# Layer scale, x + gamma * y: HBM in two blocks of 64 rows, and y's first rows on two DMA rings

## The chip, the core and the metric

The kernel runs on one core of one Trainium2 chip. The metric is the device time of one execution in microseconds (us). Before the change the median of 3 runs is 119.68 us (119.56 to 119.86).

## The reference

```python
B, S, D = 1024, 16, 512          # bf16
def reference(x, y, gamma):      # x, y: (B, S, D), gamma: (D,)
    return x + gamma * y
```

x and y are read once and the result is written once: 16.8 MB each, 50.3 MB in all.

## The kernel before

The 16,384 rows of 512 elements (1 KB each) are seen as 128 rows on each of 128 partitions. "Row" below means one such row on every partition, 128 KB in all. The whole of y lies in SBUF (`y_sb`, 128 rows a partition), and the result is made in place there. x passes through a smaller buffer, `x_sb`, of 76 rows, so the later part of x overwrites rows that have been added already.

`BLOCKS` says how HBM is cut: in a block of n rows each partition's n rows lie next to each other, so a transfer of part of a block is one contiguous run for each partition (4 rows: 4,096 B; 64 rows: 65,536 B). `PIECES` says how the rows are cut for VectorE (DVE). There is no scheduler; the lists at the top are the order:

- `SP` is what SyncE issues on its DMA ring, in order: y's rows 0 to 4, y's rows 4 to 68, x's rows 4 to 68, y's rows 68 to 128, x's rows 68 to 120, x's rows 120 to 128. The fourth number of an x entry is the row of `x_sb` where it goes.
- `ACT` is what ScalarE issues on its ring: x's rows 0 to 4, gamma (1 KB), and the three stores. ScalarE computes nothing.
- `EARLY` takes the first two entries of SP and the first of ACT ahead of the program's opening barrier (the last lines of the kernel function move these instructions to the front of the main block).
- `HOLD` and `AHEAD`: all entries of a ring after its first (2, 1) wait until the transfer `HOLD`, y's rows 0 to 4, has landed. TensorE (PE) waits for that landing and passes it on to SP, ACT and DVE.
- An x entry that overwrites rows of `x_sb` waits for the adds that read them (`frees`). In before.py x's rows 68 to 120 wait for the first add, of 44 rows, and x's rows 120 to 128 wait for the later ones.
- `RELEASE`: the first store waits, besides for its adds, until x's rows 68 to 120 have landed (`s_go`), so that nearly all reads come before all writes.
- `DVE` is the order of the multiplies (m) and adds (a) by piece. A multiply waits for the y transfers that its piece touches, an add for its x transfers.

gamma is spread over the partitions by a matmul of PE with a row of ones (line 152), and DVE casts it to bf16 (line 154). PE takes the landing of `HOLD` first, then waits for gamma. The first multiply (line 180) can't start before the cast. The adds are line 189. The DMA instructions are issued in `ring`: gamma at line 129, x at 132, y at 135, the stores at 138. Each DMA is spread over 16 DMA engines, 8 partitions each, and its landing counts 16 completions.

Of the kernel before, what the change touches and what calls it, by code (L numbers as in the profile page):

```python
# [3 lines left out]

BLOCKS = [4, 64, 60]

PIECES = [8, 16, 44, 52, 8]


SP = [
    ('y', 0, 4),
    ('y', 4, 68),
    ('x', 4, 68, 4),
    ('y', 68, 128),
    ('x', 68, 120, 24),
    ('x', 120, 128, 0),
]
ACT = [('x', 0, 4, 0), ('g',), ('s', 4, 68), ('s', 0, 4), ('s', 68, 128)]  # L20

EARLY = (2, 1)

HOLD, AHEAD = ('y', 0, 4), (2, 1)

RELEASE = ('x', 68, 120, 24)

DVE = [('m', 0), ('m', 1), ('m', 2), ('a', 2), ('a', 0), ('a', 1), ('m', 3), ('m', 4), ('a', 3), ('a', 4)]
MULT, ADD = mybir.AluOpType.mult, mybir.AluOpType.add


def _take(sem, n, eng):


    return eng.wait_ge(sem, n).then_inc(sem, -n)  # L35


def kernel(
# [18 lines left out]
    rows = N // P  # L57
    n = len(PIECES)
    assert sum(PIECES) == rows
    starts = [sum(PIECES[:c]) for c in range(n + 1)]  # L60
    dt = xf.dtype
    edges = [sum(BLOCKS[:c]) for c in range(len(BLOCKS) + 1)]
    assert edges[-1] == rows

    def rows_of(t, a, b):

        c = max(c for c in range(len(BLOCKS)) if edges[c] <= a)
        assert b <= edges[c + 1]
# [6 lines left out]
    y_sb = nc.alloc_sbuf_tensor("y_sb", [P, rows, D], dt).ap()  # L75
    x_loads = [w for w in ACT + SP if w[0] == "x"]
    y_loads = [w for w in SP + ACT if w[0] == "y"]
    stores = [w for w in SP + ACT if w[0] == "s"]
    for loads in (x_loads, y_loads, stores):
# [9 lines left out]
    s_add, s_go, s_rel, s_end, s_out = sem("s_add"), sem("s_go"), sem("s_rel"), sem("s_end"), sem("s_out")  # L89
    added = [a for kind, *a in DVE if kind == "a"]  # L90
    order = {a[0]: k for k, a in enumerate(added)}

    def meets(a, b, c, d):
        return a < d and c < b
# [4 lines left out]
    def x_at(row):  # L99
        return next(w[3] + row - w[1] for w in x_loads if w[1] <= row < w[2])  # L100
# [12 lines left out]
    def ring(eng, what, n_early, n_ahead):  # L113

        known, went = 0, False
        for k, w in enumerate(what):
            kind = w[0]
            if k == n_ahead:
                _take(s_held[eng], 1, eng)
            need = frees(w) if kind == "x" else pieces_of(w[1], w[2]) + list(w[3:]) if kind == "s" else []  # L120
            need = max((order[c] + 1 for c in need), default=0)
            if kind == "s" and not went:
                _take(s_go, 1, eng)
                went = True
            if need > known:
                eng.wait_ge(s_add, need)
                known = need
            if kind == "g":
                i = eng.dma_start(out=gamma_row, in_=gamma.unsqueeze(0)).then_inc(s_gamma, 16)
            elif kind == "x":  # L130
                to = x_sb[:, w[3] : w[3] + w[2] - w[1], :]
                i = eng.dma_start(out=to, in_=rows_of(xf, w[1], w[2])).then_inc(s_load[w], 16)
            elif kind == "y":
                r = slice(w[1], w[2])
                i = eng.dma_start(out=y_sb[:, r, :], in_=rows_of(yf, w[1], w[2])).then_inc(s_load[w], 16)
            else:
                r = slice(w[1], w[2])
                i = eng.dma_start(out=rows_of(of, w[1], w[2]), in_=y_sb[:, r, :]).then_inc(s_out, 16)
            if k < n_early:
                early.append(i.ins)  # L140

    ring(nc.sync, SP, EARLY[0], AHEAD[0])
    ring(nc.scalar, ACT, EARLY[1], AHEAD[1])

# [11 lines left out]

    _take(s_load[RELEASE], 16, nc.tensor)
    nc.tensor.sem_inc(s_go, 1)
# [4 lines left out]
    def need(loads, c):  # L163
        for w in loads:
            if w not in landed and meets(starts[c], starts[c + 1], w[1], w[2]):
                if w == RELEASE:
                    _take(s_rel, 1, nc.vector)
                elif w == HOLD:
                    _take(s_held[nc.vector], 1, nc.vector)
                else:  # L170
                    _take(s_load[w], 16, nc.vector)
                landed.add(w)

    for kind, *args in DVE:
        c = args[0]
        yt = y_sb[:, starts[c] : starts[c + 1], :]
        if kind == "m":
            need(y_loads, c)
            g = gamma_sb[:, None, :].to_broadcast([P, PIECES[c], D])
            nc.vector.tensor_tensor(out=yt, in0=yt, in1=g, op=MULT).then_inc(s_dve, 1)  # L180
            open_mults += 1
        else:
# [4 lines left out]
            at = x_at(starts[c])  # L187
            xt = x_sb[:, at : at + PIECES[c], :]
            nc.vector.tensor_tensor(out=yt, in0=xt, in1=yt, op=ADD).then_inc(s_add, 1)  # L189
# [44 lines left out]
```

## Time and profile before

| | |
|---|---|
| median of 3 runs | 119.68 us |
| span of the profiled execution (first to last instruction) | 118.2 us |
| around the span, median less span | 1.5 us |
| bytes read, written | 33.56 MB, 16.78 MB; 426 GB/s over the span |
| DMA packets | 1442 (161 of them under 512 B: mostly completions) |
| VectorE busy | 70.1 us, 59% of the span, 12 instructions |
| TensorE busy | 0.6 us, one matmul |
| granted clock | 1.000 |

The span is the one that the profile was taken from; its device time is not listed beside it, so the difference between the median of the runs and the span stands for what lies around the span.

How to read it: DMA-issuing instructions are not counted as busy time of an engine; the work of the DMA engines is seen in the line of 40 slices (busy tenths of 16 engines) and in the table of queues (packets, MB, share of 16 engines' time). A packet is counted where it starts, with all of its bytes: the slices of a stretch with 64 KB packets therefore jump up and down, though the engines work evenly. In a list of instructions SPq and ACTq are the queues that issue DMAs, and the bracket at the end of a line tells how long the engine stood idle before it and what ended that.

| transfer | ring | issued at us | us to landing |
|---|---|---|---|
| y 0 to 4 | SP | 0.0 | 3.4 |
| y 4 to 68 | SP | 0.4 | 23.4 |
| x 0 to 4 | ACT | 0.1 | 4.2 |
| x 4 to 68 | SP | 3.7 | 39.5 |
| gamma | ACT | 3.9 | |
| y 68 to 128 | SP | 4.1 | 57.3 |
| x 68 to 120 | SP | 55.4 | 21.7 |
| x 120 to 128 | SP | 57.6 | 22.0 |
| store 4 to 68 | ACT | 77.4 | 23.8 |
| store 0 to 4 | ACT | 77.8 | 22.3 |
| store 68 to 128 | ACT | 94.4 | 21.5 |

### The profile page before, as it was taken

Reading aid. Unit: us, or ns where it says so; the run is one execution under the profiler, and the core shown is the slowest. Engines: PE = TensorE matmul, PEld = TensorE weight load, DVE = VectorE, ACT = ScalarE, POOL = GpSimd, SP = SyncE. Lnnn points to the kernel's source line nnn. Section 1 sums busy time; section 2 is a strip of 40 time slices with the busy share of each in tenths; the row PEclk is TensorE's granted clock in tenths of the full one; section 3 lists DMA queues with packets and bytes.
Section 4 is the critical chain, followed back from the end, with each engine's and each line's share of the span. In section 5 each row is a group of like instructions: output and inputs, shape, how many; then the busy total and the mean of one; then the engine's idle time right before and its main releaser. Section 6 shows DMA issues by size and latency. Waiting matters only on the chain. (4 is left out here: it accounts for less than half of the span.)

```text
span 118.2 us, 91 instructions
## 1 busy us (share of the span) xinstructions
PE 0.6 (0%) x1; PEld 0.1 (0%) x1; DVE 70.1 (59%) x12; POOL 0.2 (0%) x4
## 2 busy tenths in 40 slices
PE   0000100000000000000000000000000000000000
PEld 0000000000000000000000000000000000000000
DVE  0000200089999969999999999999999900000000
POOL 0000000000000000000000000000000000000000
DMA  6999889988899879879969696898899889799793
GB/s 248 461 666 399 355 355 399 665 355 355 355 599 466 355 333 624 374 333 499 499 288 576 288 576 288 360 637 355 355 576 488 355 355 510 333 582 416 333 499 166
DMA packets 1442, 50.33 MB, mean 426 GB/s; under 512 B 161, under 2 KB 162, under 8 KB 546
## 3 DMA queue, kind: packets, MB, share of 16 engines
q1 hardware_dynamic: 864, 33.03, 64.8%
q10 hardware_dynamic: 578, 17.30, 33.9%
HBM read 33.56 MB, written 16.78 MB: 426 GB/s over the span
## 5 line engine op out<-in xcount | busy, mean ns | idle before, releaser
L180 DVE TENSOR_TENSOR y_sb<-y_sb,gamma_sb 128x4096 bf16<-128x4096 bf16 (+3 forms) x5 | 34.7, 6981 | 10.9 <-DVEq L35 10.9
L189 DVE TENSOR_TENSOR y_sb<-x_sb,y_sb 128x4096 bf16<-128x4096 bf16 (+3 forms) x5 | 34.7, 6981 | 1.2 <-DVEq L35 1.1
L154 DVE CAST gamma_sb<-gamma_ps 128x512 bf16<-128x512 f32 x1 | 0.7, 692 | 10.2 <-DVEq L35 10.2
L146 DVE MEMSET ones_row<- 1x128 bf16 x1 | 0.2, 165 | 2.0 <-PEq L51 2.0
L152 PE MATMUL gamma_ps<-gamma_row,ones_row 1*128 1x512 bf16 x1 | 0.6, 581 | 11.6 <-PEq L35 11.6
L152 PEld LDWEIGHTS gamma_ps<-gamma_row,ones_row 1*128 1x128 bf16 x1 | 0.1, 101 | 11.6 <-issue 11.6
L218 POOL MEMSET const-bfloat16-1.0<- 128x1 bf16 x1 | 0.1, 101 | 0.0
L218 POOL MEMSET const-uint8-127<- 128x1 uint8 x1 | 0.1, 101 | 0.0
L218 POOL MEMSET const-float32-0.0<- 128x1 f32 x1 | 0.1, 98 | 0.2 <-issue 0.2
L218 POOL MEMSET const-float32-1.0<- 128x1 f32 x1 | 0.1, 98 | 0.0
## 6 DMA issues: line engine op xcount, KB each, us to landing
y_sb<-in_y_dram SPq DMA_DIRECT2D x1, 7680.0 KB, 57.3
out_dram<-y_sb ACTq DMA_DIRECT2D x1, 7680.0 KB, 23.8
x_sb<-in_x_dram SPq DMA_DIRECT2D x1, 6656.0 KB, 21.7
x_sb<-in_x_dram SPq DMA_DIRECT2D x1, 1024.0 KB, 22.0
y_sb<-in_y_dram SPq DMA_DIRECT2D x1, 512.0 KB, 3.4
x_sb<-in_x_dram ACTq DMA_DIRECT2D x1, 512.0 KB, 4.2
out_dram<-y_sb ACTq DMA_DIRECT2D x1, 512.0 KB, 22.3
y_sb<-in_y_dram SPq DMA_DIRECT2D x1, 23.4
```

Source lines behind the costliest of these rows:

```text
L146: nc.vector.memset(ones_row, 1.0).then_inc(s_ones, 1)
L152: nc.tensor.matmul(gamma_ps, ones_row, gamma_row, start=True, stop=True).then_inc(s_ps, 1)
L154: nc.vector.tensor_copy(out=gamma_sb, in_=gamma_ps).then_inc(s_dve, 1)
L180: nc.vector.tensor_tensor(out=yt, in0=yt, in1=g, op=MULT).then_inc(s_dve, 1)
L189: nc.vector.tensor_tensor(out=yt, in0=xt, in1=yt, op=ADD).then_inc(s_add, 1)
L218: nc = _bacc.Bacc("TRN2", target_bir_lowering=False, num_devices=1)
```

## The change

HBM is cut in two blocks of 64 rows. y's first block comes in two transfers: its first 8 rows as the only early entry on SP's ring, its next 56 rows as the first instruction on ACT's ring, ahead of gamma. `HOLD` is y's first 8 rows. x comes in 64, 56 and 8 rows, all on SP; there are two stores of 64 rows instead of three. DVE has four pieces, 20, 44, 56 and 8 rows, instead of five. Nothing below the lists is changed; line numbers fall by one.

```diff
-BLOCKS = [4, 64, 60]
-
-PIECES = [8, 16, 44, 52, 8]
+BLOCKS = [64, 64]
+
+PIECES = [20, 44, 56, 8]
 SP = [
-    ('y', 0, 4),
-    ('y', 4, 68),
-    ('x', 4, 68, 4),
-    ('y', 68, 128),
-    ('x', 68, 120, 24),
+    ('y', 0, 8),
+    ('x', 0, 64, 0),
+    ('y', 64, 128),
+    ('x', 64, 120, 20),
     ('x', 120, 128, 0),
 ]
-ACT = [('x', 0, 4, 0), ('g',), ('s', 4, 68), ('s', 0, 4), ('s', 68, 128)]
-
-EARLY = (2, 1)
-
-HOLD, AHEAD = ('y', 0, 4), (2, 1)
-
-RELEASE = ('x', 68, 120, 24)
-
-DVE = [('m', 0), ('m', 1), ('m', 2), ('a', 2), ('a', 0), ('a', 1), ('m', 3), ('m', 4), ('a', 3), ('a', 4)]
+ACT = [('y', 8, 64), ('g',), ('s', 0, 64), ('s', 64, 128)]
+
+EARLY = (1, 1)
+
+HOLD, AHEAD = ('y', 0, 8), (1, 1)
+
+RELEASE = ('x', 64, 120, 20)
+
+DVE = [('m', 0), ('m', 1), ('a', 1), ('a', 0), ('m', 2), ('m', 3), ('a', 2), ('a', 3)]
```

What each engine waits for after the change follows from the same rules: SP's x 0 to 64 waits for the landing of y 0 to 8, with y 64 to 128 behind it; x 64 to 120 goes to rows 20 to 76 of `x_sb` and waits for the first add (piece 1, rows 20 to 64); x 120 to 128 goes to rows 0 to 8 and waits for the second add (piece 0). The first multiply needs both early y transfers and gamma.

## The prediction

> **What bounds the kernel now.** I read the page's table of queues first, then the 40 slices, then the timeline, then the packet counts of short windows.
>
> ```profile
> DMA  6999889988899879879969696898899889799793
> ...
> q1 hardware_dynamic: 864, 33.03, 64.8%
> q10 hardware_dynamic: 578, 17.30, 33.9%
> ```
>
> The columns of the two queue lines are packets, MB and share of 16 engines' span; q1 is SP's ring and q10 ACT's. Together the packets fill 98.7% of the span, so the DMA engines bound the kernel, and nothing can be gained but the 1.0 us before the first packet and some tenths of packet overhead. Much can be lost: any stretch in which both rings are empty is added to the end. So the question is whether the change opens such stretches. The packet records give the prices: a run of 4,096 B takes an engine 0.159 us, 8,192 B 0.309, 53,248 B 1.966, 61,440 B 2.267 and 65,536 B 2.418 (57,344 B, which before.py lacks, falls at 2.117 between its neighbours).
>
> Next, who else is close. The timeline:
>
> ```profile
> 3.71 0.33 SPq L132 DMA_DIRECT2D x_sb<-in_x_dram  x1
> 3.90 0.50 ACTq L129 DMA_DIRECT2D gamma_row<-in_gamma_dram  x1
> ...
> 12.32 0.69 DVE L154 CAST gamma_sb<-gamma_ps 128x512 bf16<-128x512 f32 x1 [10.16 <-DVEq L35]
> 23.95 18.43 DVE L180 TENSOR_TENSOR y_sb<-y_sb,gamma_sb 128x4096 bf16<-128x4096 bf16 x3 [10.94 <-DVEq L35]
> 43.45 18.43 DVE L189 TENSOR_TENSOR y_sb<-x_sb,y_sb 128x22528 bf16<-128x22528 bf16 x3 [1.08 <-DVEq L35]
> ```
>
> Columns: start, length, engine, line. DVE starts at 23.95, when y's first 64-row transfer lands; gamma was ready at 13.01. From there DVE stands still for only 1.08 us (x's 64 rows) and ends its last add at 94.39; the last store is issued at 94.43. The transfer ahead of that store ends near 99.6 on the engines, and a store needs 1.32 us from issue to first packet (77.41 to 78.73), so **DVE has about 3.8 us to spare**: its start may slip from 23.95 to about 27.8 before the last store is late.
>
> **How two rings share an engine.** The change puts two long transfers on two rings at the start, so I need the sharing rule. Packet counts of three windows, 1.0 to 2.2, 2.2 to 3.05 and 3.05 to 3.65 us:
>
> ```profile
> q1 hardware_dynamic: 102, 0.42, 91.9%
> ```
> ```profile
> q10 hardware_dynamic: 60, 0.25, 72.8%
> q1 hardware_dynamic: 42, 0.11, 31.4%
> ```
> ```profile
> q10 hardware_dynamic: 62, 0.25, 101.4%
> ```
>
> In the first only y's rows 0 to 4 run (102 of 128 rows). ACT's x rows, issued at 0.13, come in at 2.2. In the second, chained end to end on one engine, the records read x, y, x, completion, x: one for one. On nearly every engine seven y rows (28 KB) were through before the first x row. y's 64 rows, third in the order of issue, start only after the last x row, at 3.65.
>
> Gamma shows the same with big packets. The windows 6.0 to 8.6, 8.6 to 8.65 and 11.1 to 11.15 us:
>
> ```profile
> q1 hardware_dynamic: 19, 1.25, 111.0%
> ```
> ```profile
> q10 hardware_dynamic: 1, 0.00, 5.8%
> ```
> ```profile
> q10 hardware_dynamic: 1, 0.00, 1.1%
> ```
>
> Gamma, issued at 3.90, waits behind the 64 KB packet that began at 6.1 (taken up ahead of it), goes at 8.62, and its completion, a packet of its own, waits for one more 64 KB packet until 11.12. So engines **alternate packet by packet whatever the size**, with one packet taken up ahead.
>
> [...]
>
> **The change, part by part.** "y8" is y 0:8 on SP, "y56" is y 8:64 on ACT; x64, y64, x56, x8 follow on SP.
>
> 1. Start. y8 stands where y's 4 rows stood, so it starts at 1.0 to 1.25; y56 stands where x's 4 rows stood, so it comes in after 28 KB of y8, which is 3.5 packets of 8 KB: four packets go first, four remain. From about 2.6 on the slowest engine the order is y56, y8, y56, y8, ... : the completion of y8 comes after five 56 KB packets and four of 8 KB, 5 x 2.117 + 4 x 0.309 = 11.8 us, at 14.4. (From above: eight packets first, 4.0 us. From below: two first, 19.)
>
> 2. The hold. PE passes y8's landing on; SP's x64 waits for it, with y64 queued behind, and ACT's gamma, with the stores behind. From last completion to x64's issue it took 0.66 us (3.05 to 3.71), so x64 is issued at 15.1, gamma at 15.3 (at 3.71 and 3.90 before, where y's 64 rows stood ahead of the hold and kept SP's ring full); x64's first packet is ready 1.0 (as y's first) to 1.3 us (as the store) later, 16.1 to 16.4.
>
> 3. Gamma. It is now **behind y56 in the same ring**. At 14.4 two or three packets of y56 remain: the sixth to 16.5, the seventh (taken up ahead) to 18.6, then turns: x64 to 21.0, y56's eighth to 23.2, x64 to 25.6, y56's completion, x64 to 28.0, gamma, x64 to 30.4, gamma's completion. An engine that began earlier is 0.3 ahead: 30.3. In before.py it was 1.9 us from there to the end of the cast (11.12 to 13.01), so DVE starts at 32.2. This is the step with most in it: if y56's completion goes together with its last packet, one turn of 2.4 us less; if x64 comes in before the seventh packet, 2.4 more.
>
> 4. DVE. A row costs 0.267 us and an operation 0.143 besides ((14.021 - 11.886)/8; 11.886 - 44 x 0.267). Pieces 20, 44, 56, 8: 5.48, 11.89, 15.09, 2.29, twice, 69.5; ten operations now sum to 69.8 and take 69.3 end to end, 0.05 less each; so 69.1. Two operations fewer save 0.2. Nothing lies idle in it: x64 lands at 40.5, before 49.5 when its add can begin; y64 lands at 59.8, wanted at 67.
>
> 5. x56. It overwrites x rows 20 to 64, so it waits for the add of 44 rows: issue at 32.2 + 29.1 = 61.3, first packet 62.4. y64's last packet ends at 59.4: **the rings are empty for 3.0 us**. Before, x's 52 rows were issued at 55.37, with 5 us of y still to come: that was the cover.
>
> 6. Stores. x56 lands at 79.8, x8's packets end at 81.9, and the first 64-row store follows to 101.3. The last add ends at 32.2 + 69.1 = 101.3; the second store is issued 0.04 later and its first packet goes at 102.6: another 1.3 us empty.
>
> 7. Packets. y's 4, x's 4 and the store of 4 rows go: 24 packets of 4 KB an engine, each 0.008 us longer than its bytes cost in a 64 KB packet, 0.2 us saved; one issue fewer on SP and one on ACT lie under transfers. Blocks of 64 rows leave each partition one run of up to 64 KB, a size that before.py's x, y and store already have at 2.418 us: nothing. It costs nothing also that x_sb shrinks to the same 76 rows.
>
> Sum, along DVE: 32.2 + 69.1 + 0.04 + 1.32 + 8 x 2.418 + 0.44 (spread of the engines) + 0.38 (last completion 117.84 to the end, 118.2) = 122.8, against the profiled 118.2: 4.6 more, which the two empty stretches (4.3) and the spread explain. The median of the runs, 119.68, lies 1.46 above the profiled span; with the same beside it, **124.2 us**.
>
> **The rivals.** With r the y8 packets that are left when y56 comes in, the same steps give for DVE's start s and the time (s + 92.1 from 27.8 on):
>
> - *Three or fewer left* (y56 later, or several small packets taken up ahead): x64 comes in earlier and every further turn delays gamma. r = 3: s 34.7, 126.8; r = 2: 37.3, 129.4; all eight first: landing at 4.0, six turns of y56 against x64, s 44.4, 136.5. For it: the 2.2 us start of ACT may be a ring whose small rows were taken up ahead; against: gamma went after one packet.
> - *Five left* (four, and a packet that y56 overtakes): landing 16.6, x64 ready at 18.4 behind the eighth packet, s 30.0, 122.1.
> - *The cover holds* (not slower). With r = 6 the hold ends at 19.0 and x64 comes in just as y56 runs out, at 20.4: gamma has no turns to wait beyond two, s is 27.4, under 27.8, and the empty stretches of 5 and 6 don't exist. 0.3 us empty, 0.2 saved: 119.5 to 119.9; and down to 119.2 if the longer first packets also fill the slow start (1.00 to 3.65 moved 385 GB/s, the whole span 426: 0.25 us). It decides where y56's first packet goes by 2.0 rather than 2.6. For it: the 3.8 us that DVE has to spare; against: seven rows on almost every engine.
> - *Too late*: r = 7 or more, hold until y56 is through: 1.7 us empty at 20.4, and s 28.9: 121.0.
>
> **How the numbers follow.** Four left, 124.2 (122 to 126.7 by the turns of step 3): 0.45. Three or fewer: 0.21. Five: 0.13. Too late: 0.05. The cover holds: 0.16, of it 0.07 with the slow start filled too. A measurement of this kernel tells about 0.3% (0.36 us) from no change: faster 0.07, within 0.09, slower 0.84. The range leaves out the clear gains below and r of 1 or none above: 119.6 to 129.4.
>
> **What would show it.** In the changed profile: y8's landing at 14.4 (step 1); x64 issued at 15.1 (2); gamma's completion, and with it PE's matmul, at 30 and the first multiply at 32 (3); a slice with empty DMA at 59 to 62 and one at 101 (5, 6); the last store issued at 101. If the multiply starts before 28, the forecast falls and the time stays near 119.7. It would be wrong too if a small packet is not worth a turn, or if gamma doesn't wait for y56's last packet.

## The result and the profile after

| | before | after |
|---|---|---|
| median | 119.69 us (4 runs, 119.56 to 119.86) | 121.87 us (4 runs, 121.77 to 122.06) |
| span of the profiled execution | 118.2 us | 120.7 us (its time: 122.06) |
| GB/s over the span | 426 | 417 |
| first multiply starts | 23.95 | 30.54 |

The change makes the kernel slower: ratio 1.0181, 95% interval 1.0169 to 1.0193. On a second chip it was 122.37 us, ratio 1.0220 (1.0203 to 1.0237). The forecast was 124.2: the right sign, the time inside the range, but twice the loss (4.5 us instead of 2.2). Single executions of the experiments split4 and dial_early below differ by about 3 us among themselves; where it matters, the traced one is named.

The 40 slices and the queues of the changed kernel:

```profile
DMA  9888979988998899889399798798889888898888
...
q1 hardware_dynamic: 720, 26.21, 51.2%
q10 hardware_dynamic: 434, 24.12, 46.2%
```

The two rings together fill 97.4% of a longer span, 98.7% before: 120.7 x 2.6% = 3.1 us without a packet, 1.5 before. One slice, the twentieth (57 to 60 us), shows a 3. Packets are counted where they start, so the window 59 to 62 in 40 slices says it more sharply:

```profile
DMA  0000000000000000000000009999999000000000
```

From 59.0 to 60.8 no packet starts, and y's second block had its last packets end between 59.5 and 60.1. The next is x's 56 rows. Its issue and its causes stand in the timeline:

```profile
15.65 0.33 SPq L131 DMA_DIRECT2D x_sb<-in_x_dram  x1
15.85 0.50 ACTq L128 DMA_DIRECT2D gamma_row<-in_gamma_dram  x1
...
29.48 0.69 DVE L153 CAST gamma_sb<-gamma_ps 128x512 bf16<-128x512 f32 x1 [27.65 <-DVEq L34]
30.54 17.29 DVE L179 TENSOR_TENSOR y_sb<-y_sb,gamma_sb 128x10240 bf16<-128x10240 bf16 x2 [0.37 <-DVEq L34]
47.98 17.29 DVE L188 TENSOR_TENSOR y_sb<-x_sb,y_sb 128x22528 bf16<-128x22528 bf16 x2
59.90 5.73 SPq L131 DMA_DIRECT2D x_sb<-in_x_dram  x2
```

Gamma's cast comes at 29.48, 17 us later than before; DVE starts at 30.54 and stands still for nothing after that; the add of 44 rows ends at 59.87, and x's 56 rows are issued at 59.90 and start at 60.85, when the rings have run out.

Why gamma comes so late stands in three windows, 2.6 to 14.4, 14.4 to 15.0 and 28.2 to 28.3 us:

```profile
q10 hardware_dynamic: 80, 4.59, 89.8%
q1 hardware_dynamic: 70, 0.57, 11.5%
```
```profile
q10 hardware_dynamic: 16, 0.92, 352.8%
q1 hardware_dynamic: 16, 0.00, 1.5%
```
```profile
q10 hardware_dynamic: 1, 0.00, 0.6%
```

In the first, the 16 engines start 80 packets of y's 56 rows, five each, in turn with what is left of y's first 8 rows. In the second come the 16 completions of those 8 rows (14.46 to 14.96 us). The packet of the third is gamma's completion, at 28.24. Gamma, unlike the other transfers, is a single packet (1,024 B, at 25.78 us) on one of the 16 engines.

To say where the time went I add up the packet records: how far the 16 engines are, at a given moment, behind a steady 27.1 B/ns each (the rate of the 64 KB packets: 65,536 B in 2.418 us) counted from 1.0 us. These **arrears**, in us:

| kernel | at 4 us | 55 | 70 | 98 | 116 |
|---|---|---|---|---|---|
| before | 0.4 | 0.5 | 0.5 | 0.5 | 0.5 |
| after | 0.7 | 0.7 | 2.7 | 2.7 | 3.2 |

So of 2.7 us more (the span is 2.5 longer), 0.2 arise at the start, 2.05 around 60 us and 0.45 at 100 us, ahead of the second store. The 2.05 are two things: 1.25 without a packet, and 0.8 because the first packets after the pause are slow (one took 3.15 us; the 128 packets of x's 56 rows take 17.7 us an engine, where the same size took 16.9 in y's 56 rows).

### The profile page after: what moved, and what is told of

It reads as the page before. It is cut to its first block, busy times and chain, and to the rows that moved or that the text cites. A ratio compares the mean times of both kernels' runs of the same rounds, so it can differ in the third digit from the quotient of the medians.

```text
span 120.7 us, 86 instructions
## 1 busy us (share of the span) xinstructions
PE 0.6 (0%) x1; PEld 0.1 (0%) x1; DVE 69.9 (58%) x10; POOL 0.2 (0%) x4
## 5 line engine op out<-in xcount | busy, mean ns | idle before, releaser
L179 DVE TENSOR_TENSOR y_sb<-y_sb,gamma_sb 128x10240 bf16<-128x10240 bf16 (+3 forms) x4 | 34.6, 8686 | 0.4 <-DVEq L34 0.4
L188 DVE TENSOR_TENSOR y_sb<-x_sb,y_sb 128x22528 bf16<-128x22528 bf16 (+3 forms) x4 | 34.6, 8688 | 0.3
```

## The experiments

Theory A: gamma, behind y's 56 rows on ACT's ring, waits for turns of long packets, so the first multiply comes late; through the first add x's 56 rows come late, and the rings run dry. Rival B: the blocks, pieces, longer first packets and two stores cost the time. Rival C: the pause at 60 us is a loss by itself. Rival D: the number of turns is not what sets gamma's landing. The experiments come from four chips; each ratio is against the kernel before on the same chip. In the expectation of before_dve_late7 the letter B, and in that of hold_on_y56 the letter C, stands for another rival, which is said there.

**Gamma to the other ring.**

```diff
 SP = [
     ('y', 0, 8),
+    ('g',),
     ('x', 0, 64, 0),
...
-ACT = [('y', 8, 64), ('g',), ('s', 0, 64), ('s', 64, 128)]
+ACT = [('y', 8, 64), ('s', 0, 64), ('s', 64, 128)]
```

> The changed kernel with one entry moved: gamma goes to SP's ring, after y's first 8 rows and ahead of x's 64 rows, instead of behind y's 56 rows on ACT's ring. Theory A (gamma's turns behind y's 56 rows delay the first multiply from 24 to 30.5 us, and through it x's 56 rows and the last store): gamma's completion comes by 21 to 24 us, the first multiply starts at 23 to 25.5, x's 56 rows are issued before y's second block ends, no stretch with empty rings is left; time 119.5 to 120.0. Rival B (the blocks, the longer first packets and the pieces cost the time, the order of gamma doesn't): 121.6 to 122.1 as in the changed kernel.

Measured: 120.39 us, ratio 1.0057 (1.0040 to 1.0073). Its timeline:

```profile
16.18 0.30 SPq L129 DMA_DIRECT2D gamma_row<-in_gamma_dram  x1
...
24.75 17.29 DVE L180 TENSOR_TENSOR y_sb<-y_sb,gamma_sb 128x10240 bf16<-128x10240 bf16 x2 [1.26 <-DVEq L35]
...
54.11 5.73 SPq L132 DMA_DIRECT2D x_sb<-in_x_dram  x2
```

Gamma is issued no earlier, but the first multiply starts 5.8 us earlier, and now waits for y's 56 rows (the 1.26 in the bracket). x's 56 rows are issued at 54.11 and the pause is gone: arrears 1.08 at 4 us and 1.06 at 116, nothing added on the way. By the ratios (1.0181 and 1.0220 against 1.0057) that one entry of the list is worth 1.5 to 2.0 us (the changed kernel was not run beside it); the time came out 0.4 us above the expected range, by what the start costs.

**y's 56 rows back to SP's ring**, all else as changed (`SP` begins y 0 to 8, y 8 to 64; `ACT` is gamma and two stores; `EARLY` and `AHEAD` are (2, 0)).

> The changed kernel with y's 56 rows moved back to SP's ring, right behind y's first 8 rows and ahead of the barrier as those; ACT has gamma and the two stores. Blocks, pieces and stores stay as changed. Theory A: y's 8 rows land near 4 us, gamma alternates with y's 56 KB packets and completes near 12, the first multiply waits for y's 56 rows alone and starts near 21.5; the add of 44 rows waits for x until about 40.5, nothing is late; time 119.2 to 119.7. Rival B: the blocks and pieces cost it, 121.6 to 122.1.

Measured: 119.88 us, ratio 1.0010 (0.9995 to 1.0025): no difference from before that can be measured. First multiply at 21.88. Blocks of 64 rows, four pieces, two stores and 8 KB first packets therefore cost nothing that shows: **rival B falls**. What costs is y's 56 rows on ACT's ring, ahead of gamma. The time is 0.2 above the expected range.

**The add of 44 rows first.**

```diff
-DVE = [('m', 0), ('m', 1), ('a', 1), ('a', 0), ('m', 2), ...
+DVE = [('m', 1), ('a', 1), ('m', 0), ('a', 0), ('m', 2), ...
```

> The changed kernel with DVE's first four operations in the order m1, a1, m0, a0 instead of m0, m1, a1, a0: the add of 44 rows, which x's 56 rows wait for, ends 5.5 us earlier, and the start of DVE (30.5) and the end of its last add (99.9) stay. Theory A, with two limits in series: the empty stretch at 60 us goes (1.2 us and a slow first packet), the first store starts some 2 us earlier, but the second store still waits for the last add, so a stretch of about 2 us opens ahead of it: 121.5 to 121.9, no gain. Rival C (the empty stretch before x's 56 rows is the whole loss and its removal is kept): 119.7 to 120.1.

Measured: 122.60 us, ratio 1.0238 (1.0222 to 1.0255), no better than the changed kernel. SP's last issues and the window 98 to 102 of this kernel:

```profile
54.95 11.37 SPq L131 DMA_DIRECT2D x_sb<-in_x_dram  x2
```
```profile
DMA  0000000000000000000000000000000000999000
```

x's 56 rows go out at 54.95 and the pause at 60 closes (arrears 1.1 up to 70 us). But the last add still ends at 100.6, the second store starts at 101.5, and the engines run out of packets between 98.8 and 99.5: the arrears jump from 1.2 to 3.9 there. **Rival C falls**: the end of DVE's chain sets the time, and a pause that is closed earlier opens again ahead of the last store. The time is 0.7 us above the range expected; the late start was later here too (31.00, y's 8 rows having landed 0.8 later).

**Only DVE late, in the kernel before.** Three extra multiplies of 8 rows, into rows of the x buffer that are free then:

```diff
             g = gamma_sb[:, None, :].to_broadcast([P, PIECES[c], D])
+            for _ in range(3 if c == 0 else 0):
+                nc.vector.tensor_tensor(out=x_sb[:, 68:76, :], in0=yt, in1=g, op=MULT).then_inc(s_dve, 1)
+                _take(s_dve, 1, nc.vector)
```

> The kernel before with three extra multiplies of 8 rows ahead of the first multiply (into 8 rows of the x buffer that are free then): they only hold DVE back by some 7.0 us, so its chain of work stands as if it began at 31.0 instead of 23.95; rings, blocks and pieces are those of before. Theory A: a late DVE alone gives the loss: x's 52 rows are issued near 61.3, after y's last block, rings empty for over 1 us with a slow restart, the last store is issued near 100.4; time 121.5 to 122.1. Rival B: DVE's start doesn't matter by itself, under 120.2.

Measured: 123.27 us, ratio 1.0290 (1.0274 to 1.0306).

```profile
24.23 7.17 DVE L181 TENSOR_TENSOR x_sb<-y_sb,gamma_sb 128x4096 bf16<-128x4096 bf16 x3 [10.97 <-DVEq L35]
31.54 18.43 DVE L183 TENSOR_TENSOR y_sb<-y_sb,gamma_sb 128x4096 bf16<-128x4096 bf16 x3
...
62.03 2.53 SPq L132 DMA_DIRECT2D x_sb<-in_x_dram  x2
```

The first column shows the real work starting at 31.54, 7.6 us late, and x's 52 rows at 62.03 instead of 55.37. Arrears 0.7 up to 55 us, 3.8 at 70. A late DVE alone gives the loss, with the rings as before. The time is 1.2 us above the expected range: the work started 0.5 us later than expected, and the engines stood empty for 2.5 us on average where I expected "over 1", besides 0.55 us of slow first packets.

**Only a little late**: one extra multiply instead of three (`range(1 ...)`).

> The kernel before with one extra multiply of 8 rows ahead of the first multiply instead of three: DVE is 2.3 us later, less than the 3.8 us that it has to spare. Theory A: no change, 119.6 to 120.0. A rival in which every delay of DVE goes to the end: 121.0 to 122.0.

Measured: 119.78 us, ratio 1.0003 (0.9993 to 1.0014), with the first multiply at 26.66. The 2.7 us are swallowed; 7.6 are not. That DVE has a few us to spare is shown, not only argued.

**The changed kernel again**, beside the next two.

> The changed kernel itself, so that the next three stand beside it on one chip. 121.6 to 122.6; first multiply at 30.5 to 31.0.

Measured: 122.37 us; first multiply at 30.75.

**The split at row 4, and at row 12** (`('y', 0, 4)` and `('y', 4, 64)`, then 12, with `HOLD` to match).

> The changed kernel with the split of y's first block at row 4 instead of 8: y 0 to 4 on SP (4 KB packets), y 4 to 64 on ACT (60 KB packets). Theory A (packets take turns, so the landing of y's first rows, and with it x's 64 rows, comes after as many long packets as short ones are left when ACT's ring comes in at 2.7): one short packet left, landing near 7.6, x's 64 rows take turns with five or more long packets and gamma stands behind all of them: gamma's completion near 35, first multiply near 37.7, time 128.5 to 130.5. Rival B (the blocks and longer packets cost it, the split row does not matter): 121.6 to 122.6.

> The changed kernel with the split at row 12: y 0 to 12 on SP (12 KB packets), y 12 to 64 on ACT (52 KB packets). Theory A: three short packets go first, five are left, the landing comes after six long packets at 17.0 to 17.5, x's 64 rows come in when only the last long packet is left, gamma's completion near 26, first multiply near 28: no empty stretch at 60 us to speak of, time 119.8 to 120.6. Rival B: 121.6 to 122.6.

| split | long packets ahead of the landing | x's 64 rows issued | first multiply | time, ratio |
|---|---|---|---|---|
| 4 | 2 | 9.16 | 40.88 | 129.85, 1.0834 (1.0816 to 1.0852) |
| 8 | 5 | 16.10 | 30.75 | 122.37, 1.0220 (1.0203 to 1.0237) |
| 12 | 6 | 18.53 | 28.18 | 121.78, 1.0157 (1.0123 to 1.0192) |

In these three traces, the earlier y's first rows land, the later the first multiply starts: of y's eight long packets an engine, six, three and two are at that landing still to come, ahead of gamma in ACT's ring. The row of the split alone moves the time by 8 us. The ratio of split 4 leaves out its traced execution, 132.39 us, to which the 9.16 and the 40.88 belong; the other three (129.60 to 129.96) are not traced. One turn more of x on gamma's engine would make most of the 2.6 us between them, but that is not shown. Split 12 missed its range by 1.2 us and lies inside that of rival B, so its time alone doesn't decide between the two; split 4 and y56_on_sp do. Its first multiply came when expected and its trace (121.02 us, the shortest of its four) shows a pause of only 0.2, but arrears of 1.0 at the start and 0.35 more at 80 us; what its other three executions had more is not traced.

**The hold on y's 56 rows instead of y's 8** (`HOLD, AHEAD = ('y', 8, 64), (1, 1)`), on one chip with the kernel before and the next one.

> The kernel before, for a trace from the same chip as the next two. 119.6 to 120.0.

119.85 us; arrears 0.55 at 4 us, 0.7 from 20 us to the end.

> The changed kernel with the hold on y's 56 rows (ACT) instead of y's first 8 rows: x's 64 rows and gamma are issued only when y's whole first block has landed, so neither takes turns with it. Theory A (turns, and a price for every stretch in which the rings are empty): x's 64 rows are issued near 22, rings empty for 2.0 to 2.5 us and a slow restart of 0.5 to 0.8, gamma completes by 26.5, first multiply before 28.5, no empty stretch later: 122.4 to 123.4, so no better than the changed kernel although gamma comes earlier. Rival C (what costs time is the turns of x against y, an empty stretch this early is made up later): 120.0 to 121.0.

Measured: 123.25 us, ratio 1.0277 (1.0260 to 1.0295). Window 20 to 27 of this kernel:

```profile
DMA  0000000000000000000099900900000000000099
```

x's 64 rows are issued at 22.64 and start at 23.60, the rings having run out at 20.9 to 21.9; their first packets take up to 3.5 us, and the arrears go from 1.1 to 4.1. This early pause is not made up later. Gamma came later than I expected, behind a slow packet of x (first multiply at 31.41), which cost nothing more, since everything after the pause is late by the same 3 us.

**One transfer of 64 rows and no hold.** `SP` begins `('y', 0, 64), ('x', 0, 64, 0)`, `ACT` is gamma, early, and two stores; `HOLD, AHEAD = ('y', 0, 64), (3, 1)`.

> The changed kernel without the split and the hold at the start: y's first 64 rows are one early transfer on SP, x's 64 rows follow in the same ring without waiting, gamma is ACT's early entry. Blocks, pieces and the two stores stay as changed. Theory A: gamma completes within 10 us, y's 64 rows land near 21.5, first multiply near 23, no empty stretch; what is left is the start, where 64 KB packets meet an idle ring (0.5 to 0.8 us instead of 0.5): 119.6 to 120.2, equal to before within the measurement or nearly. Rival B (blocks, pieces and two stores cost time): over 121.0.

Measured: 120.06 us, ratio 1.0024 (1.0011 to 1.0036). First multiply at 24.45, no pause; arrears 0.85 at the start (64 KB packets meet an idle ring: one took 3.4 us), 0.9 at the end. Within 0.3% of before without any of the care about the first rows. No version here beats the kernel before.

**Only x's issue earlier.** This is the test of the step that failed (see below). SP's hold is released by DVE after five dummy multiplies, not by y's landing:

```diff
     nc.vector.memset(ones_row, 1.0).then_inc(s_ones, 1)
+    s_dial = sem("s_dial")
+    nc.vector.memset(x_sb[:, 64, :], 1.0).then_inc(s_dial, 1)
+    _take(s_dial, 1, nc.vector)
+    for k in [8, 8, 8, 8, 8]:
+        row = x_sb[:, 64, :][:, None, :].to_broadcast([P, k, D])
+        nc.vector.tensor_tensor(out=x_sb[:, 65 : 65 + k, :], in0=row, in1=row, op=MULT).then_inc(s_dial, 1)
+        _take(s_dial, 1, nc.vector)
+    nc.vector.sem_inc(s_held[nc.sync], 1)
...
-    for s_one in s_held.values():
-        nc.tensor.sem_inc(s_one, 1)
+    for eng, s_one in s_held.items():
+        if eng is not nc.sync:
+            nc.tensor.sem_inc(s_one, 1)
```

> The changed kernel with one difference: SP's hold is released not by the landing of y's 8 rows but by DVE, which is idle then, after five dummy multiplies of 8 rows (into rows of the x buffer that are free until x's 56 rows come), at about 14.2 us. x's 64 rows are issued near 14.3 instead of 15.65 to 16.1; gamma is released as before. Theory A (it was a race of x's first packet against y's eighth long packet, lost by tenths): now x goes ahead of that packet on nearly every engine, x's first packets start near 18.7 to 19.5, gamma's completion comes one turn later, 30.4 to 31, first multiply near 33, time 123.8 to 125.0. Rival D (the number of turns doesn't depend on when x comes in, gamma simply waits less than two full turns): 121.7 to 122.6.

Measured: 124.64, 124.93, 125.01 and 121.91 us; the first is the traced one. Three lie in the range of theory A or on its edge. The fourth lies in rival D's; it is not traced, and which way its engines went is not known. So the reading rests on the trace.

```profile
14.82 0.33 SPq L131 DMA_DIRECT2D x_sb<-in_x_dram  x1
...
33.13 17.29 DVE L188 TENSOR_TENSOR y_sb<-y_sb,gamma_sb 128x10240 bf16<-128x10240 bf16 x2 [0.37 <-DVEq L34]
```

x is issued at 14.82, some 1 us earlier than in the changed kernel, and DVE starts **2.6 us later**. The window 18.9 to 20.1 of this kernel, then 19.1 to 20.5 and 20.7 to 21.5 of the changed one (columns: packets, MB, share):

```profile
q1 hardware_dynamic: 15, 0.98, 188.9%
```
```profile
q1 hardware_dynamic: 1, 0.07, 10.8%
```
```profile
q1 hardware_dynamic: 15, 0.98, 283.9%
```

Each of these q1 packets is a first 64 KB packet of x on one of the 16 engines. Here x goes ahead of y's last long packet on 15 engines; in the changed kernel on one, and on the other 15 it comes after.

**x's issue late**: the same with `[8, 8, 8, 8, 8, 8, 8, 2]`.

> The same with seven dummy multiplies of 8 rows and one of 2, so that x's 64 rows are issued near 19.6. Theory A: x becomes ready near 21.0, as y's 56 rows run out; gamma, which stands behind them, meets an empty SP ring and completes within 22, first multiply before 24.5; rings empty for at most 0.5 us: 120.0 to 120.9. Rival D: gamma still completes near 28, 121.7 to 122.6.

Measured: 122.64 us, ratio 1.0233 (1.0181 to 1.0285).

```profile
20.52 0.33 SPq L131 DMA_DIRECT2D x_sb<-in_x_dram  x1
...
23.51 17.29 DVE L188 TENSOR_TENSOR y_sb<-y_sb,gamma_sb 128x10240 bf16<-128x10240 bf16 x2 [0.37 <-DVEq L34]
```

The half on gamma came as expected: it passed at 21.05 without a turn, and DVE started at 23.51, so **rival D falls** on both sides. The half on the time didn't: x was issued 0.9 later than meant, its first packets took up to 3.5 us and left the engines 2 us apart (x's 64 rows end between 41.5 and 43.8), arrears 0.9 to 2.4 at 26 us; and another 1.0 came at 80 us, where the first store waits for the slowest engine's landing while the fast ones stand idle. The trace is that of the slowest of four executions (121.86 to 123.17). The time, at the edge of rival D's range, would not have told; gamma's landing does. And an early gamma alone does not save the time: the pause of the rings at 20 us, its slow restart and the wait at 80 us cost as much.

## Why the prediction was right and wrong

| step | forecast | the changed kernel |
|---|---|---|
| 1 y56 packets ahead of y8's last completion | 5 | 5 |
| 1 the last completion | 14.4 | 14.96 |
| 2 x64 issued | 15.1 | 15.65 |
| 2 x64 ready after its issue | 1.0 to 1.3 | about 1.4 (inferred below) |
| **3 gamma's completion** | **30.3** | **28.24** |
| 3 first multiply | 32.2 | 30.54 |
| 4 DVE from there to the last add's end | 69.1 | 69.4 |
| 5 rings empty before x56 | 3.0 | 1.25, and 0.8 of slow packets |
| 6 second store, issue to first packet | 1.32 | 0.85 |
| 6 rings empty before it | 1.3 | 0.4 |
| span | 122.8 | 120.7 |

**Right**: the mechanism, but for one choice in step 3. The 8 KB packets of y8 took turns one for one with the 56 KB packets of y56: of the 128 packets of y8, 64 had gone when y56's first packets started (2.67 to 3.17 us), four an engine as forecast, and y8 landed only after five long packets, its completions at 14.46 to 14.96 us; gamma, behind y56 in its ring, waited for turns with x; the late DVE made x56 and the second store late, in series. gamma_on_sp, before_dve_late7 and a1_first show each link. Step 7's nothing for the blocks is shown by y56_on_sp, within 0.25%.

**Wrong: step 3, by one turn of 2.4 us**, and with it nearly all of the miss of 2.1 in the span (2.3 in the time, since the traced execution, 122.06, is the slowest of four). I had "the seventh (taken up ahead) to 18.6, then turns: x64 to 21.0, y56's eighth to 23.2". In the trace 15 of 16 engines went from the seventh to the eighth, and only then to x. The step put a transfer that would be ready at 16.1 to 16.4 against a choice that, in these traces, falls when the seventh packet starts, with some tenths in hand. x was ready at about 17.07 (the two engines that start their seventh packet at 17.07 and 17.08 went different ways), 1.4 after its issue, while gamma's engine started its seventh at 16.7. after_again agrees: x was issued at 16.10, the 13 engines that took the eighth first had started their seventh by 17.43, and two of the three that took x first had done so at 17.46 and 17.53. The pieces of that: y8's landing 0.55 later than I had, a latency of 1.4 instead of 1.0 to 1.3, and the spread of the engines (0.5 us), which I had counted for the end and not for the choice: the release waits for the slowest engine, but gamma lies on a faster one. dial_early put x back into time: x ahead on 15 engines, gamma's completion at 30.81 where 30.3 was forecast, and 124.6 to 125.0 us in three of four executions, where 124.2 was forecast. One thing there stays open: the sixteenth engine started its seventh packet at 16.94, 2.1 us after x's issue, and still took the eighth first, so x was not ready equally soon on every engine.

I had named this turn ("if x64 comes in before the seventh packet, 2.4 more"), but only one way round; the case that came true, x64 after the eighth, was under the rival "five left", at 122.1 us, with the right start of DVE (30.0) for the wrong reason: four were left, as forecast. The range, which took the turns in, held the time, but at 9.8 us it was wide.

The smaller terms of the sum nearly cancel: the 0.4 us from the end of the cast to the first multiply, which it left out, and 0.3 more in DVE's chain, against 0.5 less from the second store's issue to its first packet (0.85, on empty rings; the 1.32 was read where x's last rows still ran) and 0.2 less at the end. The pause at 60 us is no term of the sum, which goes along DVE; it was shorter than forecast since DVE started 1.7 us earlier, and it was priced as empty time alone, though the dry ring also restarted slowly (0.8). The start cost more than before, where one rival had allowed for a gain. That is shown by size (arrears at 4 us: 0.7 to 1.25 in the nine traces with y's long transfer on ACT's ring, 0.4 to 0.7 in the four with before.py's start, 0.73 with y56 on SP's), and why it is so stays open.

## What to carry to other kernels

A small transfer that everything waits for must not stand behind a long one in the same ring: here gamma, behind y's 56 rows on ACT's ring and with SP's ring at work, waited for whole packets of both, 2.1 to 2.4 us each, and on SP's ring (gamma_on_sp) the first multiply started 5.8 us earlier. When a wait on a landing decides when another ring comes in, work out the choice for the engine that matters, with its own start and the slowest one's release: here 0.4 us (x ready at 17.07, gamma's engine at its seventh packet at 16.7) moved a whole packet. And a wait on the way is worth looking at only together with the last one on the same engine; in a1_first closing the first, at 60 us, only moved the loss to 100 us.

## What the runs showed of the hardware

- In six kernels (the changed one, before_dve_late7, split4, hold_on_y56, dial_early, dial_late) a ring that had run dry cost more than the pause: the first packets after it took up to 3.0 to 3.5 us where 2.0 to 2.4 is steady, 0.55 to 0.8 us an engine. In dial_late the engines came out of it 2 us apart, which cost again, 1.0 us, at the next wait for a landing. All six are loads. The second stores of the changed kernel and of a1_first, on engines that had been empty for 0.4 and 2.6 us, show no such price: their first packets took 2.45 to 2.46 us, where 2.42 is steady.
- In the changed kernel the completion of a transfer is a packet of its own (4 B, 0.009 us) and waits for a turn: y56's came one x packet after its last data (23.2 against 20.8), gamma's one x packet after gamma (28.24 against 25.78).
- In the kernel before the three transfers issued first came in one after the other, at 1.0, 2.2 and 3.65 us, though issued within half a microsecond.
